# Dealing the prepared projection's steps by its handovers, and two more PSUM banks for the last logits

## The chip, the cores and the metric

One core of one Trainium2 chip runs the whole program. The metric is device time in microseconds of one launch, as the median of repeated runs. The engines are named as in the profile: PE (TensorE matmuls), PEld (its weight loads), DVE (VectorE), ACT (ScalarE), POOL (GpSimd), SP (SyncE, which issues most DMAs and passes some waits on).

## The reference

The input x has 2048 rows of 512 numbers. Four layers follow each other, A, B, A, B, each as `x = x + layer(layernorm(x))`, with 32 heads of 16 numbers. What matters here is layer B: attention inside four segments of 512 rows, with a memory that is carried from segment to segment.

```
def _A_ref(x, wqkv, w_phi, wo):          # linear attention with a learned feature map
    q, k, v = split(x @ wqkv)
    phi(t) = concat(softmax(t @ w_phi), softmax(-(t @ w_phi)))
    o = phi(q) (phi(k)^T v) / (phi(q) sum(phi(k)) + 1e-6)
    return o @ wo

def _B_ref(x, wq, wk, wv, wo, beta):
    for s in range(4):                   # segments of 512 rows
        qs, ks, vs = q[:, :, s], k[:, :, s], v[:, :, s]
        logits = einsum("bhqd,bhkd->bhqk", qs, ks) * scale + mask    # causal
        a_dot = softmax(logits) @ vs
        a_mem = (phi(qs) @ M) / (phi(qs) @ z + 1e-6)
        outs.append(g * a_mem + (1.0 - g) * a_dot)
        M = M + phi(ks)^T vs;  z = z + sum(phi(ks))
    return concat(outs) @ wo
```

## The kernel before

The kernel keeps float32 values as two parts, a high part rounded to the matmul's type and a low rest (hi and lo; hh and hl, oh and ol are such pairs), and multiplies three of the four combinations. Every instruction is issued from helpers, so line numbers are those of the helpers: L154 for DVE, ACT, POOL and SP, L176 for matmuls (`mm`), L180 for transposes (`tp`). Instructions run on each engine in the order in which the program writes them.

Layer B (`class LayerB`) works in 32 groups m, four heads of one segment each, and `steps` runs through them in rounds of a loop over k. A group takes R = 5 rounds; k = 0 to 159 are the rounds proper. In each round:

- `attend` puts the logits of one part of group m = k // 5 into PSUM, exponentiates them on ACT into a tile P (six buffers), and has POOL set the entries beyond the diagonal to zero (`affine_select`). The logits take two banks, one for each half e of the rows; the tile is `lg`, and there is one of it. It is 4 matmuls for the rounds k % 5 = 2, 3 and 4, and 2 for the others.
- `maxima` does the products from which the maxima of a later group are taken, into the banks `mx` and `my` (or two of the four `g` buffers). It runs LEAD = 9 rounds ahead, so the last of it is before k = 151. The last transposed maxima (`put_maxima`) use `mx` at k = 150.
- at k % 5 = 0, `weighted` multiplies the tiles P of the group before by v (`g<-P,v`), and `finish` brings an earlier group's result back to rows.

Beside this, each round has a slot of other work from a table, one per kind of segment: FIRST, GAPS, and for the last segment LAST (first layer B) or FINAL (second layer B). An entry such as `6.2 P/6` stands for k = 120 + 6·5 + 2 = 152 and means six steps of the generator `early`. A `v/1` in LAST is one step of the following layer A's first pass.

`early` is the prepared projection: the last segment's rows are projected with wo for the three quarters of the heads that are done, so that only the last quarter is left behind the loop. It goes in two halves of two row tiles each. A half is `pre` or `pt` steps (loads, transposes, the pair oh and ol from them, in two buffers each), and then 18 steps of `mm3_pair`. A step is two matmuls side by side, one on rows 0 to 63 of the array and one on rows 64 to 127. The two halves of the rows take turns at the two banks: steps 1 to 4 one way, 5 to 13 the other, 14 to 18 the first way again. At such a change the first matmul waits for the last of the turn before. This goes through SP, as a no-operation that waits for the matmul and signals back:

```
                if first and step > 0 and row == 0:
                    after(i, passed)
            if step + 1 < len(steps) and steps[step + 1][4]:
                passed = sync.nop(nofuse=True)
                after(passed, i)
```

These are the handovers: behind the 4th and the 13th step of each half. In the table before, a slot of six steps (k = 152, 153, 154) has the first handover inside the slot of 152 and the second inside that of 154. At k = 156 to 159 the slots had 4, 5, 5 and 4 steps in LAST and 4, 3, 3 and 2 in FINAL, where the last six steps come behind the loop: four behind the last group's `finish`, the others behind the transposes of `end_turn`, which then casts into the same two buffers oh. `thin` is true in the second layer B alone.

Of the kernel before, what the change touches and what calls it, by code (L numbers as in the profile page):

```python
# [10 lines left out]
AF = mybir.ActivationFunctionType  # L11
# [7 lines left out]
P = 128  # L19
NSEG = 4  # L20
# [12 lines left out]
R = 5  # L33
# [46 lines left out]
3.0 max turn turn fin ln | 3.1 O/6     | 3.2 O/6           | 3.3 O/6 | 3.4 O/6  # L80
4.0 max ln ln a2 fin a2 | 4.1 v/2      | 4.2 v/2           | 4.3 v/2 | 4.4 v/2
5.0 max a3 a3 fin | 5.1 v/2           | 5.2 v/2           | 5.3 v/2 | 5.4 v/2
6.0 max fin pre | 6.1 pt pt         | 6.2 P/6           | 6.3 P/6 | 6.4 P/6 v/1
7.0 max pt pt fin | 7.1 P/4           | 7.2 P/5 v/1       | 7.3 P/5 v/1 | 7.4 P/4 v/2
"""
FINAL = """
0.0 max a1 a1 fin | 0.1 Q2/6          | 0.2 Q2/6          | 0.3 Q2/6 | 0.4 Q2/6
# [2 lines left out]
3.0 max a2 a2 fin | 3.1 O/6           | 3.2 O/6           | 3.3 O/6 | 3.4 O/6  # L90
4.0 max turn turn fin | 4.1 O/6        | 4.2 O/6           | 4.3 O/6 | 4.4 O/6
5.0 max a3 a3 fin | 5.1 O/6           | 5.2 O/6           | 5.3 O/6 | 5.4 O/6
6.0 max fin pre | 6.1 pt pt         | 6.2 P/6           | 6.3 P/6 | 6.4 P/6
7.0 max pt pt fin | 7.1 P/4           | 7.2 P/3           | 7.3 P/3 | 7.4 P/2
"""
BEFORE = {-25: "load q0", -24: "sq0 sq1", -23: "k0", -22: "sk0 n n", -21: "sk1 v0/2 n n", -20: "v0/2 n n",
          -19: "n n", -18: "v1 n n q1/2", -17: "q1/2", -16: "k1/2", -15: "k1/2", -11: "v2", -9: "max0"}
# [3 lines left out]
def interleave_kernel(ctx, tc, x_in, a_wqkv, a_wphi, a_wo, b_wq, b_wk, b_wv, b_wo, b_beta,  # L101
# [13 lines left out]
    def nm(s):  # L115
        uid[0] += 1
        return f"{s}_{uid[0]}"

    def T2(tag, bufs, dt=F32, shape=(P, 512)):
        return sp.tile(list(shape), dt, tag=tag, bufs=bufs, name=nm(tag))  # L120

    def PS(tag, bufs, shape=(P, 512)):
        return ps.tile(list(shape), F32, tag=tag, bufs=bufs, name=nm(tag))
# [38 lines left out]
    dve, act, pool, sync = [Ordered(e) for e in (nc.vector, nc.scalar, nc.gpsimd, nc.sync)]  # L162

    def held(i):

        if last[0] is not None:
            behind(i, last[0])
        last[0] = i
        return i
# [3 lines left out]
    def mm(*a, **k):  # L173
        n = a[0].free_size()
        work[0] += n / 2.26 if k["rhs"].dtype == F32R else (n * 2 / 2.4 + 25 if "tile_position" in k else 2 * max(112, n * 2 / 2.4))
        return held(nc.tensor.matmul(*a, **k))  # L176
# [803 lines left out]
    class LayerB:  # L980
# [211 lines left out]
        def attend(self, m):  # L1192


            s, c, hf = m // 8, m % 8 // 2, m % 2
            Q, K = [t[:, 2 * hf : 2 * hf + 2, :] for t in self.st[s, c]["set"]]
            self.pr[m] = {}

            def prod(pb, r, kb, at, w):
                for e in range(2):  # L1200
                    q, k = Q[64 * e : 64 * e + 64, r, :], K[64 * e : 64 * e + 64, r, :]
                    mm(pb[:, e, at : at + w], lhsT=k[:, kb * P : (kb + 1) * P],
                       rhs=q[:, 512 - w : 512], start=True, stop=True, tile_position=(64 * e, 0))

            for kbs, r in (((0,), 0), ((0,), 1), ((1, 3), 0), ((1, 3), 1), ((2,), None)):
                pb = PS("lg", 1, (P, 2, 512))
                pr = T2("P4", NP4, shape=(P, 2, 512))
                pq = pr.rearrange("p e (b x) -> p e b x", b=4)
                if kbs == (0,):
                    prod(pb, r, 0, 0, 512)  # L1210
                    diags = [pr[:, :, 0:P]]
                elif kbs == (1, 3):
                    prod(pb, r, 3, 256, 256)
                    prod(pb, r, 1, 0, 384)
                    diags = [pq[:, e, 0:4:3, :] for e in range(2)]
                else:
                    for rr in range(2):
                        prod(pb, rr, 2, 256 * rr, 256)
                    diags = [pr.rearrange("p e (r x) -> p (e r) x", r=2)[:, :, 0:P]]
                self.pr[m][kbs, r] = pr  # L1220
                with tc.high_priority():
                    act.activation(pr, pb, AF.Exp, scale=0.25)
                for diag in diags:
                    pool.affine_select(out=diag, in_=diag, pattern=[[0, diag.shape[1]], [1, P]],
                                            compare_op=ALU.is_ge, fill=0.0, base=0, channel_multiplier=-1)
                yield
# [327 lines left out]
```

## Time and profile before

| | |
|---|---|
| median of 3 runs | 1360.74 us (1359.96 to 1362.49) |
| profiled execution | 1361.73 us |
| its span, first to last instruction | 1360.0 us |
| PE busy | 1317.2 us, 97% of the span |
| DVE, ACT, POOL busy | 76%, 59%, 51% |
| exponentials of logits, P<-lg | 320 of 1030 ns each |
| granted PE clock, mean | 0.999 |

A row of a timeline gives the start in us from the span's beginning, the time that the row covers, the engine, the line, the operation, output<-input, and in brackets the idle time of the engine ahead of it with what released it. Rows that are alike and follow each other are merged (x4). A matmul's own duration is longer than the distance to the next one, since they overlap in the array; distances between starts are what PE's throughput is read from. In the chain that ended last, "issue" is time in which the engine waited for nothing that the profile shows. The end of the first layer B's loop lies at about 670 to 695 us, that of the second at 1327 to 1347.

### The profile page before, as it was taken

What the parts mean: (1) busy time and instruction counts of PE and PEld (TensorE: products, weight loads), DVE (VectorE), ACT (ScalarE), POOL (GpSimd) and SP (SyncE); (2) the same over time, 40 slices, a digit from 0 to 9 for tenths busy, and PEclk for the clock granted to TensorE, in tenths of its full rate; (3) what the DMA queues carried; (4) which work ended last, traced back from release to release, by engine and by line L of the source; (5) the groups of instructions that cost most, each with busy time, mean ns of one, the idle gap of its engine ahead of it and who ended that gap; (6) DMA issues with size and microseconds to landing.
All of it is one profiled execution on the core that took longest, in us unless ns stands there. A gap on an engine that the chain in (4) does not pass through costs nothing.

```text
span 1360.0 us, 36811 instructions
## 1 busy us (share of the span) xinstructions
PE 1317.2 (97%) x14056; PEld 1028.9 (76%) x14056; DVE 1040.3 (76%) x3256; ACT 808.7 (59%) x1201; POOL 696.9 (51%) x1060
## 2 busy tenths in 40 slices
PE   7999989999999999999999998999999999999997
PEld 6888868777777877777768886786777787787764
DVE  4766778777888888888657677887778879878882
ACT  5556345547677677677544433453766866866654
POOL 1568666326447557345324356553356656654442
PEclk9999999999999999999999999999999999999999
DMA  6388447535654544546251103755555554544441
GB/s 205 102 325 278 157 132 231 173 97 140 173 167 131 158 117 134 153 120 182 87 181 37 63 33 126 241 164 132 143 163 164 152 157 99 150 130 98 118 116 42
DMA packets 134400, 196.27 MB, mean 144 GB/s; under 512 B 15440, under 2 KB 61648, under 8 KB 133456
## 3 DMA queue, kind: packets, MB, share of 16 engines
q1 hardware_dynamic: 132256, 193.27, 48.8%
q8 instruction: 112, 1.84, 0.6%
q10 hardware_dynamic: 1968, 0.64, 0.2%
q14 instruction: 64, 0.52, 0.1%
HBM read 101.05 MB, written 39.85 MB: 104 GB/s over the span
## 4 chain that ended last, share of the span: by engine, by line
PE 76%; DVE 11%; ACT 4%; issue 3%; POOL 3%; DMA 1%; SPq 0%; ACTq 0%; DVEq 0%; POOLq 0%
PE g L176 58%; PE lg L176 6%; PE g L180 6%; PE mx L176 3%; ACT P L154 2%; POOL P L154 2%; DVE g L154 2%; PE lg L180 2%; PE my L176 1%; DVE es L154 1%; POOL tb L154 1%; DVE my L154 1%; DVE mx L154 1%; DVE mxs L154 1%; PE mx L180 1%
## 5 line engine op out<-in xcount | busy, mean ns | idle before, releaser
L154 ACT ACTIVATE P<-lg 128x1024 f32<-128x1024 f32 x320 | 329.6, 1030 | 171.4 <-PE lg L176 93.8
L154 POOL TENSOR_SCALAR_AFFINE_SELECT P<-P 128x256 f32<-128x256 f32 (+1 forms) x448 | 193.4, 446 | 285.7 <-ACT P L154 284.0
L154 DVE CUSTOM_DVE_ANT_0 g<-g,mask 128x256 f32<-128x256 f32 (+3 forms) x392 | 191.6, 545 | 8.6 <-PE g L176 8.3
L176 PE MATMUL g<-hh,wqk 64*128 64x512 f32 (+1 forms) x960 | 186.5, 392 | 0.5 <-DMA wqk<-wqk 0.3
L176 PE MATMUL g<-w,oh 64*128 64x512 f32 (+2 forms) x880 | 177.7, 384 | 1.3 <-DVE ol L154 0.7
L154 DVE CUSTOM_DVE_ANT_0 mx<-mx,mask 128x512 f32<-128x512 f32 (+2 forms) x316 | 158.0, 500 | 21.3 <-PE my L176 17.6
L154 DVE CUSTOM_DVE_ANT_0 my<-my,mask 128x512 f32<-128x512 f32 (+2 forms) x316 | 164.1, 519 | 0.0
L176 PE MATMUL lg<-e,e 64*128 64x256 f32 (+2 forms) x1024 | 153.1, 339 | 4.1 <-ACT P L154 4.1
L176 PE MATMUL g<-P,v 128*32 128x128 f32 (+3 forms) x2064 | 151.1, 433 | 3.6 <-DVE mxs L154 3.0
L176 PE MATMUL g<-w,hh 64*128 64x512 f32 (+1 forms) x672 | 143.9, 395 | 2.0 <-ACT w L154 1.3
L154 DVE DVE_READ_ACCUMULATOR2_ANT mxs<- 128x1 f32 x1024 | 145.3, 142 | 0.0
L176 PEld LDWEIGHTS lg<-e,e 64*128 64x128 f32 x1024 | 102.1, 185 | 35.2 <-issue 11.3
L176 PEld LDWEIGHTS g<-P,v 128*32 128x32 f32 x2064 | 61.2, 109 | 87.5 <-issue 60.8
L176 PEld LDWEIGHTS g<-w,oh 64*128 64x128 f32 (+1 forms) x880 | 107.0, 186 | 18.5 <-SPq L154 3.0
L176 PEld LDWEIGHTS g<-hh,wqk 64*128 64x128 f32 (+1 forms) x960 | 105.6, 185 | 17.2 <-PE my L176 1.0
L154 POOL TENSOR_SCALAR tb<-tb 128x512 f32<-128x512 f32 x72 | 109.2, 1528 | 16.0 <-ACT tb L154 16.0
L176 PE MATMUL g<-w,ol 64*128 64x512 f32 (+2 forms) x440 | 115.6, 377 | 0.0
L176 PE MATMUL g<-hl,wqk 64*128 64x512 f32 (+1 forms) x480 | 106.2, 391 | 0.2
L176 PEld LDWEIGHTS g<-w,hh 64*128 64x128 f32 (+1 forms) x672 | 84.4, 187 | 16.1 <-ACT w L154 1.6
L154 ACT COPY tb<-g 128x512 f32<-128x512 f32 (+1 forms) x132 | 71.2, 576 | 42.7 <-PE g L176 40.8
L176 PE MATMUL g<-w,hl 64*128 64x512 f32 (+1 forms) x336 | 90.1, 392 | 0.0
L154 DVE TENSOR_REDUCE es<-P 128x64 f32<-128x1024 f32 x64 | 77.4, 1209 | 12.9 <-ACT P L154 12.9
(149 smaller groups left out, 2887.9 us busy)
## 6 DMA issues: line engine op xcount, KB each, us to landing
e<-ta SPq DMA_DIRECT2D x384, 128.0 KB
wqk<-wqk SPq DMA_DIRECT2D x128, 256.0 KB
x<-x SPq DMA_DIRECT2D x48, 256.0 KB
ot<-in SPq DMA_DIRECT2D x26, 256.0 KB
pq<-tb SPq DMA_DIRECT2D x24, 256.0 KB
tb<-pq SPq DMA_DIRECT2D x24, 256.0 KB
x<-xr SPq DMA_DIRECT2D x22, 256.0 KB
xr<-x SPq DMA_DIRECT2D x20, 256.0 KB
```

The lines of the kernel that those rows point to most:

```text
L154: i = f(*a, **k)
L176: return held(nc.tensor.matmul(*a, **k))
L180: return held(nc.tensor.transpose(*a))
```

## The change

The slots of the last two blocks in LAST and FINAL get other numbers of steps: 4, 9 and 5 at k = 152, 153 and 154 in both. At k = 156 to 159 LAST has 4, 5, 4 and 5, and FINAL 4, 5, 4 and none. So each handover now falls between two slots, with the logits of the next round written in between. In FINAL 13 steps instead of 12 lie inside the loop.

In the second layer B, the rounds k = 153, 155, 157 and 159 put their logits into `mx` and `my` instead of `lg`, and exponentiate the two banks by two instructions of 512 elements each.

```
-6.0 max fin pre | 6.1 pt pt         | 6.2 P/6           | 6.3 P/6 | 6.4 P/6 v/1
-7.0 max pt pt fin | 7.1 P/4           | 7.2 P/5 v/1       | 7.3 P/5 v/1 | 7.4 P/4 v/2
+6.0 max fin pre | 6.1 pt pt         | 6.2 P/4           | 6.3 P/9 | 6.4 P/5 v/1
+7.0 max pt pt fin | 7.1 P/4           | 7.2 P/5 v/1       | 7.3 P/4 v/1 | 7.4 P/5 v/2
...
-7.0 max pt pt fin | 7.1 P/4           | 7.2 P/3           | 7.3 P/3 | 7.4 P/2
+7.0 max pt pt fin | 7.1 P/4           | 7.2 P/5           | 7.3 P/4 | 7.4
...
-                    mm(pb[:, e, at : at + w], lhsT=k[:, kb * P : (kb + 1) * P],
+                    mm(pb[e][:, at : at + w], lhsT=k[:, kb * P : (kb + 1) * P],
...
-                pb = PS("lg", 1, (P, 2, 512))
+                apart = self.thin and self.k > 8 * R * NSEG - 9 and self.k % 2
+                if apart:
+                    pb = [PS(t, 1) for t in ("mx", "my")]
+                else:
+                    both = PS("lg", 1, (P, 2, 512))
+                    pb = [both[:, e] for e in range(2)]
...
-                    act.activation(pr, pb, AF.Exp, scale=0.25)
+                    for out, src in ([(pr[:, e], pb[e]) for e in range(2)] if apart else [(pr, both)]):
+                        act.activation(out, src, AF.Exp, scale=0.25)
```

On PE, in the first layer B at k = 158 and 159, the handover (from the rows `w_4966,ol` to the rows `w_4967,oh` of the prepared projection, tiles g_10432 and g_10433) stood ahead of layer A's step (g_10465) and the logits lg:

```order
 L176 MATMUL g_10433<-w_4966,ol_10403 128x512
 L176 MATMUL g_10432<-w_4966,ol_10401 128x512
-L176 MATMUL g_10432<-w_4967,oh_10400 128x512
-L176 MATMUL g_10433<-w_4967,oh_10402 128x512
 L176 MATMUL g_10465<-e_1898_10365,hh_9449 128x512
 L176 MATMUL g_10465<-e_1899_10366,hh_9449 128x512
 L176 MATMUL g_10465<-e_1898_10365,hl_9450 128x512
-L176 MATMUL lg_10505<-e_450_2824,e_451_2825 128x256 x4
+L176 MATMUL lg_10503<-e_450_2824,e_451_2825 128x256 x4
+L176 MATMUL g_10432<-w_4967,oh_10400 128x512
+L176 MATMUL g_10433<-w_4967,oh_10402 128x512
```

The step behind the handover has moved behind the logits.

On PE, in the second layer B at k = 152 and 153, the same with the new banks; the first handover is where g_20165 is followed by g_20165 again:

```order
 L176 MATMUL g_20164<-w_14902,oh_20139 128x512
-L176 MATMUL g_20165<-w_14902,oh_20141 128x512 x2
+L176 MATMUL g_20165<-w_14902,oh_20141 128x512
+L176 MATMUL mx_20175<-e_2263_12760,e_2264_12761 128x256
+L176 MATMUL my_20176<-e_2263_12760,e_2264_12761 128x256
+L176 MATMUL mx_20175<-e_2263_12760,e_2264_12761 128x384
+L176 MATMUL my_20176<-e_2263_12760,e_2264_12761 128x384
+L176 MATMUL g_20165<-w_14902,oh_20141 128x512
 L176 MATMUL g_20164<-w_14902,oh_20139 128x512
```

The logits of k = 153 now stand at the handover, in mx and my.

On PE, behind the second loop, from the middle of the leftover steps to the first matmul of the last quarter (before; tmp are the last heads' rows that `end_turn` transposes):

```order
-L176 MATMUL g_20280<-w_14902,oh_20248 128x512
-L176 MATMUL g_20281<-w_14902,oh_20250 128x512
-L180 MATMUL g_20390<-ident,tmp_19924 128x128 x2
-L180 MATMUL g_20397<-ident,tmp_19924 128x128 x2
-L176 MATMUL g_20280<-w_14903,oh_20248 128x512
-L176 MATMUL g_20281<-w_14903,oh_20250 128x512
-L176 MATMUL g_20280<-w_14902,ol_20249 128x512
-L176 MATMUL g_20281<-w_14902,ol_20251 128x512
-L176 MATMUL g_20406<-w_14902,oh_20388 128x512
```

The same place in the changed kernel:

```order
+L176 MATMUL g_20284<-w_14903,oh_20252 128x512
+L176 MATMUL g_20285<-w_14903,oh_20254 128x512
+L180 MATMUL g_20400<-ident,tmp_19924 128x128 x2
+L180 MATMUL g_20407<-ident,tmp_19924 128x128 x2
+L176 MATMUL g_20284<-w_14902,ol_20253 128x512
+L176 MATMUL g_20285<-w_14902,ol_20255 128x512
+L176 MATMUL g_20414<-w_14902,oh_20398 128x512
```

The last step that reads the old oh (`w_14903,oh`) has moved from behind the transposes to ahead of them; one step is left behind them.

More of the change, by code (lines that the diff above doesn't have):

```diff
@@ L92 @@
 5.0 max a3 a3 fin | 5.1 O/6           | 5.2 O/6           | 5.3 O/6 | 5.4 O/6
-6.0 max fin pre | 6.1 pt pt         | 6.2 P/6           | 6.3 P/6 | 6.4 P/6
-7.0 max pt pt fin | 7.1 P/4           | 7.2 P/3           | 7.3 P/3 | 7.4 P/2
+6.0 max fin pre | 6.1 pt pt         | 6.2 P/4           | 6.3 P/9 | 6.4 P/5
+7.0 max pt pt fin | 7.1 P/4           | 7.2 P/5           | 7.3 P/4 | 7.4
 """
```

## The prediction

> **What bounds the kernel now.** I read the page first, for the shares and the chain that ended last, then the chain in order of time, then the timelines of TensorE (PE), its weight loads, ScalarE (ACT) and VectorE (DVE) at the ends of the two loops.
>
> ```profile
> PE 1317.2 (97%) x14056; PEld 1028.9 (76%) x14056; DVE 1040.3 (76%) x3256; ACT 808.7 (59%) x1201; POOL 696.9 (51%) x1060
> PE 76%; DVE 11%; ACT 4%; issue 3%; POOL 3%; DMA 1%; SPq 0%; ACTq 0%; DVEq 0%; POOLq 0%
> ```
>
> PE is busy 97% of the span and carries 76% of the chain, so a stretch can only be shortened where PE waits. The first such place is the last block of rounds (k = 156 to 159). The chain there is logits, exponential, logits, exponential:
>
> ```profile
> 1342.46 1.03 ACT P L154
> ...
> 1343.54 0.58 PE lg L176 x4
> ...
> 1344.23 1.03 ACT P L154
> ```
>
> One turn from exponential to exponential takes 1344.23 - 1342.46 = 1.77 us, because the next logits go into the one pair of banks (lg) that the exponential is still reading. PE has less work than that per round:
>
> ```profile
> 1340.12 0.50 PE L176 MATMUL lg<-e,e 64*128 64x512 f32 x2
> ...
> 1341.24 0.59 PE L176 MATMUL g<-w,oh 64*128 64x512 f32 x2
> 1341.80 0.56 PE L176 MATMUL lg<-e,e 64*128 64x256 f32 x4
> 1342.20 0.63 PE L176 MATMUL g<-w,oh 64*128 64x512 f32 x4
> 1342.66 0.41 PE L176 MATMUL g<-w,ol 64*128 64x512 f32 x2
> 1343.54 0.56 PE L176 MATMUL lg<-e,e 64*128 64x256 f32 x4 [0.47 <-ACT P L154]
> ...
> 1344.40 0.39 PE L176 MATMUL g<-w,ol 64*128 64x512 f32 x2
> 1345.31 0.51 PE L176 MATMUL lg<-e,e 64*128 64x256 f32 x4 [0.51 <-ACT P L154]
> 1345.65 0.63 PE L176 MATMUL g<-w,oh 64*128 64x512 f32 x4
> 1346.21 2.37 PE L176 MATMUL g<-P,v 128*32 128x256 f32 x48
> ```
>
> A step of the prepared projection is two matmuls side by side; steps follow each other every 0.23 us (1342.20 to 1342.66 is two). So k = 158's logits could start at 1342.66 + 0.23 = 1342.89 and start at 1343.54: 0.65 us lost. k = 159's lose 1345.31 - 1344.63 = 0.68. k = 157's lose some 0.2.
>
> The second place is the handover inside a step pair, where the halves change banks through a wait that SyncE passes on:
>
> ```profile
> 1334.00 0.44 PE L176 MATMUL lg<-e,e 64*128 64x256 f32 x4
> 1334.28 0.39 PE L176 MATMUL g<-w,ol 64*128 64x512 f32 x2
> 1334.77 0.50 PE L176 MATMUL g<-w,oh 64*128 64x512 f32 x2
> 1335.11 0.40 PE L176 MATMUL g<-w,ol 64*128 64x512 f32 x2
> ```
>
> From the last step before it to the first behind it is 0.49 us instead of 0.23, and the next step follows after 0.34 instead of 0.23, since the array has run empty. A handover in the open costs 0.26 + 0.11, about 0.36 us. These are the ones in the open at both ends; the weight loads show what they waited for:
>
> ```profile
> 675.91 0.30 PEld L176 LDWEIGHTS g<-w,oh 64*128 64x128 f32 x4 [0.53 <-SPq L154]
> 678.96 0.19 PEld L176 LDWEIGHTS g<-w,oh 64*128 64x128 f32 x2 [0.42 <-SPq L154]
> 690.11 0.19 PEld L176 LDWEIGHTS g<-w,oh 64*128 64x128 f32 x2 [0.52 <-SPq L154]
> ```
>
> ```profile
> 1331.73 0.30 PEld L176 LDWEIGHTS g<-w,oh 64*128 64x128 f32 x4 [0.53 <-SPq L154]
> 1334.77 0.19 PEld L176 LDWEIGHTS g<-w,oh 64*128 64x128 f32 x2 [0.41 <-SPq L154]
> ```
>
> The third place is the tail behind the loop, where a handover and the leftover steps stand between the last head's transposes and the casts:
>
> ```profile
> 1349.60 0.51 PE L176 MATMUL g<-w,ol 64*128 64x512 f32 x2
> 1350.20 0.50 PE L176 MATMUL g<-w,oh 64*128 64x512 f32 x2
> ...
> 1351.09 0.66 PE L180 MATMUL g<-ident,tmp 128*128 128x128 f32 x4
> 1351.68 0.50 PE L176 MATMUL g<-w,oh 64*128 64x512 f32 x2
> 1352.02 0.39 PE L176 MATMUL g<-w,ol 64*128 64x512 f32 x2
> 1353.10 0.73 PE L176 MATMUL g<-w,oh 128*128 128x512 f32 x2 [0.69 <-DVE ol L154]
> ```
>
> ```profile
> 1352.21 0.65 ACT L154 CAST oh<-g 128x256 fp32r<-128x256 f32 x2 [3.03 <-PE g L176]
> ```
>
> ```profile
> 1350.39 0.29 DVE L154 TENSOR_TENSOR tmp<-tmp,wt 128x128 f32<-128x128 f32 x1
> ...
> 1352.62 0.76 DVE L154 TENSOR_TENSOR ol<-g,oh 128x256 fp32r<-128x256 f32 x2 [1.93 <-ACT oh L154]
> ```
>
> The cast waits for PE g of L176, not for the transposes (L180): there are two buffers oh, and the step at 1351.68 (ending 1352.18) is the last that reads the old oh. The next matmuls, at 1353.10, wait for the ol that follows the cast.
>
> **The change part by part.** First, the deal of steps in the first loop's end (times near 680). The number of matmuls is the same; only places change. The handovers at 675.91, 678.96 and 690.11 move behind the next round's logits. Those take 0.29 us on PE (1334.00 to 1334.28) after the last step's 0.23: 0.52, and the handover needs 0.49, so the cover just holds; without it 0.36 each comes back. Gain 3 x 0.36 = 1.08. One thing is late next: k = 155's logits come 0.72 earlier, but k = 154's exponential, still on lg, comes only some 0.1 earlier, and takes back about 0.18. Sum: -0.90. SyncE's order is unchanged; the eight loads of the next pass's weights that stand in its queue behind the second handover are released earlier with it. After this loop PE runs on with few waits, so the gain should arrive at the end; bounds 0 and 1.08.
>
> Second, block 6 of the second loop (k = 152 to 154): handovers at 1331.73 and 1334.77 go the same way. Here k = 153 and 155 write to mx and my, whose last use by the maxima lies before k = 151, so no logits wait. Gain 2 x 0.36 = 0.72; bounds 0.5 and 0.8.
>
> Third, block 7 (k = 156 to 159). Without waits PE would save 0.2 + 0.65 + 0.68, some 0.3 more because logits in a stream take 0.29 and not the 0.40 of 1341.80 to 1342.20, and pay 0.23 for a thirteenth step: 1.5 net. The selections on POOL come late next. In times of before less 0.72: k = 157's logits at 1340.85, its five steps from 1341.22 (the handover's 0.49 behind the fourth), k = 158's logits at 1342.39, their exponential from about 1342.94 to 1343.97, then these two kinds of selection:
>
> ```profile
> 1345.32 0.77 POOL L154 TENSOR_SCALAR_AFFINE_SELECT P<-P 128x256 f32<-128x256 f32 x2 [1.00 <-ACT P L154]
> 1347.03 0.64 POOL L154 TENSOR_SCALAR_AFFINE_SELECT P<-P 128x512 f32<-128x512 f32 x1 [0.94 <-ACT P L154]
> ```
>
> The first ends near 1344.80; the weighting (g from P and v) needs it 0.56 after its start, an estimate from 12 of its 48 matmuls in 2.37 us. It would be there at 1344.5, so it waits 0.3: at that matmul 1344.84 against 1346.77 before, 1.93 less. The second ends near 1345.8, before its matmuls at 1346.0. Less the 0.72 above, this block gives -1.20; bounds 0.5 and 1.5.
>
> Splitting four exponentials in two costs ACT little by the nearest row, two 512-wide casts that follow each other:
>
> ```profile
> 1303.82 1.03 ACT L154 CAST oh<-g 128x512 fp32r<-128x512 f32 x2
> ```
>
> That is the 1.03 of one 1024-wide exponential. I take 0.05 per split, hidden where ACT waits for PE; the upper bound is 0.4, if the halves do not overlap, and then the last selection would hold the weighting by some 0.3, inside the bounds above.
>
> The Trainium skill (ScalarE: Activation LUTs, What ACT_TABLE_LOAD costs) speaks against a split: an ACTIVATE with immediate operands costs a fixed 186 ns beside its elements, of which about 93 ns overlaps with the next. By that each pair costs 0.09 us more than one; k = 158's exponential still starts by its logits, so the sum would be the same within 0.1. The exponential of 1.03 us agrees with the page's 1.04 for 1024 elements; no run here yet shows a split.
>
> Fourth, the tail. Five steps are left instead of six, and the handover lies behind us: the four steps ahead of the transposes lose the 0.6 - 0.23 of 1349.60 to 1350.20, so the transposes start 0.36 earlier, as the last tmp on DVE (1350.39 + 0.29 = 1350.68) just allows. Behind them only an ol step is left. The first cast no longer waits for it, but the first ol does: with transposes at 1350.73 on the old scale, that step runs 1351.32 to 1351.82, ol follows at 1351.87 and not 1352.62. Gain -0.75; bounds 0.36 (the handover alone) and 1.0 (ol free too). What follows (twelve matmuls, four additions, stores) moves with it.
>
> Sum: -0.90 - 0.72 - 1.20 - 0.75 = -3.57 us. The profiled execution took 1361.73 and would take 1358.2 (span 1356.4); it lies 1 us above the median of the runs, 1360.74, from which the forecast goes: 1357.2.
>
> **The rivals.** (1) The first loop's gain is swallowed before the end, because something later is paced by DMA. For it: eight weight loads follow in SyncE's queue. Against: the page gives DMA 1% of the chain. Then -2.67: 1358.1.
>
> (2) The last block is held by ACT and POOL, at the low bounds of the third and fourth parts (0.5, 0.36): -0.90 - 0.72 - 0.50 - 0.36 = -2.5: 1358.3.
>
> (3) The change does not do what it says: PE still waits in block 7 as now, since the cover of 0.52 against 0.49 fails and the split exponentials hold mx as long as lg was held. Then only the first loop, block 6 and the tail's 0.36 remain: -2.0: 1358.8.
>
> (4) Slower. The instruction streams of ACT and PE get longer in the last rounds, and a wait for issue could fall into the last block, where nothing covers it. Such waits stand in the trace elsewhere:
>
> ```profile
> PE my L176 <- issue: 3.9, 2, 2.2
> ```
>
> Two of the longest, 4.4 us, turn the sum to +0.8: 1361.6; with three it is slower beyond doubt, 1363.8. It decides from 1.6 stalls on. Against it: both lie in another stage, none in any of the last rounds.
>
> **How the numbers follow.** About 0.2%, 2.7 us, is what a measurement of this kernel can tell from no change; three runs of before lie 2.5 apart. Chances: forecast 0.60, (1) 0.15, (2) 0.12, (3) 0.08, (4) 0.05. The line at 1358.0 runs close to (1) and (2): of the forecast 0.56 falls below it, of (1) to (3) 0.12. Faster 0.68, same 0.27, slower 0.05. The range takes the upper bounds (-1.08 - 0.8 - 1.5 - 1.0 = -4.4, 1356.4) with half a microsecond of spread, and upward reaches past (3): 1355.9 to 1359.6.
>
> **What would show it.** In the profile of the changed kernel: no weight load of these steps waits for SPq in either end; logits under mx and my at odd rounds from k = 153 with no idle time behind ACT; one short wait for POOL inside the last weighting; the last cast released by the transposes of L180, ol by the step behind them; block k = 156 to the weighting about 4.6 us instead of 6.1. Wrong would be: idle time before lg or mx of over 0.3 us in that block, a cast that still waits for L176, or the second layer starting no earlier than now.

## The result, and the profile after

| | before | changed | ratio, 95% interval |
|---|---|---|---|
| first measurement, 9 runs each | 1362.44 us | 1358.73 us | 0.9971 [0.9962, 0.9981] |
| second measurement, 21 and 12 runs | 1362.07 us | 1360.16 us | 0.9984 [0.9975, 0.9994] |
| profiled execution, span | 1361.73, 1360.0 us | 1357.14, 1355.4 us | |

The changed kernel is faster by two to three thousandths. The forecast was 1357.2 us, 3.57 us less than before. The two intervals overlap between 0.9975 and 0.9981, which is 2.6 to 3.4 us. The first measurement's medians lie 3.71 us apart, nearer to 3.57 than the parts of the change add up to below, 3.08; so that nearness is partly luck.

The page of the changed kernel, busy time of PE and shares of the chain, moves little beside that of before:

```profile
PE 1315.4 (97%) x14056; PEld 1032.6 (76%) x14056; DVE 1039.5 (77%) x3256; ACT 808.6 (60%) x1205; POOL 695.8 (51%) x1060
PE 74%; DVE 10%; ACT 5%; issue 4%; POOL 3%; DMA 3%; SPq 1%; ACTq 0%; DVEq 0%; POOLq 0%
```

What is to be seen are the four more instructions on ACT, the split exponentials. The two profiled spans lie 4.6 us apart, and that is not all the change. These are PE's timelines around the changed stretches (start, time covered, engine, line, operation, output<-input, shapes, count). First before, at the first loop's end, then its rows in the second loop that were not shown yet (the count of the weighting is cut by the window):

```profile
674.03 1.10 PE L176 MATMUL g<-w,oh 64*128 64x512 f32 x4
...
694.40 1.93 PE L176 MATMUL g<-P,v 128*32 128x512 f32 x24
...
1329.85 1.11 PE L176 MATMUL g<-w,oh 64*128 64x512 f32 x4
...
1348.51 0.44 PE L180 MATMUL g<-ident,U 128*128 128x128 f32 x2
```

Then the changed kernel, at the same places:

```profile
671.83 1.11 PE L176 MATMUL g<-w,oh 64*128 64x512 f32 x4
...
691.40 2.36 PE L176 MATMUL g<-P,v 128*32 128x512 f32 x32
...
1327.54 1.11 PE L176 MATMUL g<-w,oh 64*128 64x512 f32 x4
...
1331.38 0.39 PE L176 MATMUL g<-w,ol 64*128 64x512 f32 x2
1331.61 0.40 PE L176 MATMUL lg<-e,e 64*128 64x256 f32 x4
1331.88 0.50 PE L176 MATMUL g<-w,oh 64*128 64x512 f32 x2
1332.21 0.39 PE L176 MATMUL g<-w,ol 64*128 64x512 f32 x2
1332.44 0.63 PE L176 MATMUL g<-w,oh 64*128 64x512 f32 x4
...
1337.22 0.50 PE L176 MATMUL lg<-e,e 64*128 64x512 f32 x2
...
1340.30 0.45 PE L176 MATMUL lg<-e,e 64*128 64x256 f32 x4
...
1341.84 2.87 PE L176 MATMUL g<-P,v 128*32 128x256 f32 x48
1344.64 0.44 PE L180 MATMUL g<-ident,U 128*128 128x128 f32 x2
...
1347.42 0.50 PE L176 MATMUL g<-w,ol 64*128 64x512 f32 x2
1348.51 0.74 PE L176 MATMUL g<-w,oh 128*128 128x512 f32 x2 [0.58 <-DVE ol L154]
```

The first changed instruction comes after 674.03 in the one and 671.83 in the other: 2.20 us of the difference arise where both kernels issue the same instructions. Between the loops (694.40 to 1329.85, 691.40 to 1327.54) the changed kernel takes 636.14 instead of 635.45, 0.69 more. Neither belongs to the change. What does can be cut into four stages, from start to start of the same matmuls:

| stage | before | changed | difference | forecast |
|---|---|---|---|---|
| A: first loop, first step at k = 152 to the last weighting | 20.37 | 19.57 | -0.80 | -0.90 |
| B: second loop, first step at k = 152 to k = 156's logits | 10.27 | 9.68 | -0.59 | -0.72 |
| C: from there to the transposes of U | 8.39 | 7.42 | -0.97 | -1.20 |
| D: from there to the last quarter's first matmul | 4.59 | 3.87 | -0.72 | -0.75 |
| sum | 43.62 | 40.54 | -3.08 | -3.57 |

-3.08 - 2.20 + 0.69 = -4.59: the spans' difference is accounted for. Behind stage D nothing moves: from the last quarter's first matmul to the end of the program it is 6.88 to 6.91 us in every trace of this case. Of the time before, -3.08 us is 0.23%, a ratio of 0.9977, inside the first interval and inside the second.

Now the engines beside PE in the changed kernel's last block and tail: the weight load that waits, ACT, DVE and POOL.

```profile
1341.84 0.72 PEld L176 LDWEIGHTS g<-P,v 128*32 128x32 f32 x14
1342.79 1.44 PEld L176 LDWEIGHTS g<-P,v 128*32 128x32 f32 x34 [0.22 <-POOL P L154]
```

```profile
1329.55 0.60 ACT L154 ACTIVATE P<-mx 128x512 f32<-128x512 f32 x1 [0.75 <-PE mx L176]
1330.04 0.59 ACT L154 ACTIVATE P<-my 128x512 f32<-128x512 f32 x1
...
1340.88 1.03 ACT L154 ACTIVATE P<-lg 128x1024 f32<-128x1024 f32 x1 [0.62 <-PE lg L176]
1342.01 0.60 ACT L154 ACTIVATE P<-mx 128x512 f32<-128x512 f32 x1
...
1347.31 0.65 ACT L154 CAST oh<-g 128x256 fp32r<-128x256 f32 x2 [2.03 <-PE g L180]
```

```profile
1348.03 0.76 DVE L154 TENSOR_TENSOR ol<-g,oh 128x256 fp32r<-128x256 f32 x2 [1.22 <-PE g L176]
```

```profile
1341.97 0.76 POOL L154 TENSOR_SCALAR_AFFINE_SELECT P<-P 128x256 f32<-128x256 f32 x2 [1.24 <-ACT P L154]
1343.22 0.63 POOL L154 TENSOR_SCALAR_AFFINE_SELECT P<-P 128x512 f32<-128x512 f32 x1 [0.49 <-ACT P L154]
```

In this stretch (the second loop's last two blocks and the tail) the view of waits, which counts waits above 0.15 us, has no weight load behind SPq and no matmul into lg, mx or my behind ACT: both of the losses that the prediction read are gone there. ACT, which before came round once in 1.77 us, now runs k = 158's and 159's exponentials almost one into the other (1340.88 + 1.03 = 1341.91, next at 1342.01). What ends last in the block is POOL's selection: it ends at 1341.97 + 0.76 = 1342.73, and the weight loads go on at 1342.79. In the tail the cast is released by the transposes (L180), and ol by the one step behind them.

### The profile page after: what moved, and what is told of

Read it like the earlier page. It is cut to its first block, busy times and chain, and to the rows that moved or that the text cites. A ratio compares the mean times of both kernels' runs of the same rounds, so it can differ in the third digit from the quotient of the medians.

```text
span 1355.4 us, 36817 instructions
## 1 busy us (share of the span) xinstructions
PE 1315.4 (97%) x14056; PEld 1032.6 (76%) x14056; DVE 1039.5 (77%) x3256; ACT 808.6 (60%) x1205; POOL 695.8 (51%) x1060
## 4 chain that ended last, share of the span: by engine, by line
PE 74%; DVE 10%; ACT 5%; issue 4%; POOL 3%; DMA 3%; SPq 1%; ACTq 0%; DVEq 0%; POOLq 0%
PE g L176 56%; PE lg L176 6%; PE g L180 6%; PE mx L176 3%; ACT P L154 3%; POOL P L154 2%; DVE g L154 2%; PE lg L180 2%; SPq L154 1%; POOL tb L154 1%; PE my L176 1%; DMA x<-x 1%; DVE es L154 1%; PE mx L180 1%; DVE my L154 1%
## 5 line engine op out<-in xcount | busy, mean ns | idle before, releaser
L154 ACT ACTIVATE P<-lg 128x1024 f32<-128x1024 f32 x316 | 325.4, 1030 | 167.1 <-PE lg L176 92.5
L176 PE MATMUL lg<-e,e 64*128 64x512 f32 (+1 forms) x1010 | 152.0, 339 | 3.1 <-ACT P L154 3.1
```

The lines of the kernel that those rows point to most:

```text
L154: i = f(*a, **k)
```

## The experiments

A total of one run says little here, since executions of the same program lie up to 7 us apart (before, in one measurement of 35 runs: 1358.86 to 1365.79 us). The stages do say something: a stage is taken from each trace as above, from start to start of the same matmuls.

| kernel | A | B | C | D | sum against before | ratio from the sum | measured ratio |
|---|---|---|---|---|---|---|---|
| before, again | 20.37 | 10.27 | 8.39 | 4.59 | 0.00 | 1.0000 | 1.0002 [0.9990, 1.0015] |
| first loop's deal alone | 19.56 | 10.26 | 8.39 | 4.59 | -0.82 | 0.9994 | 0.9993 [0.9982, 1.0005] |
| second loop's deal alone | 20.36 | 9.85 | 8.17 | 3.88 | -1.36 | 0.9990 | 0.9994 [0.9982, 1.0006] |
| banks alone | 20.38 | 10.21 | 6.96 | 4.57 | -1.50 | 0.9989 | 0.9988 [0.9977, 1.0000] |
| changed, again | 19.60 | 9.69 | 7.42 | 3.87 | -3.04 | 0.9978 | 0.9984 [0.9975, 0.9994] |
| two amendments | 19.57 | 9.69 | 6.96 | 3.56 | -3.84 | 0.9972 | 0.9974 [0.9963, 0.9984] |
| three amendments | 19.27 | 9.69 | 6.96 | 3.56 | -4.14 | 0.9970 | 0.9969 [0.9957, 0.9981] |

The measured ratios follow the sums. Only the intervals of the lower four end at a ratio of 1 or below it; for the two deals by themselves the totals cannot be told from before, and the stages have to decide.

**The kernel before, once more.** No edit.

> The kernel before, unchanged, as a control of the timing and of the granted clock from run to run. Theory (four local gains, and single executions that differ by a couple of microseconds for reasons that have nothing to do with the change): a ratio of 1 within 0.1 to 0.15%, and clocks between 0.995 and 0.999, as the changed kernel's runs had. Rival (the changed kernel costs clock: its runs show 0.995 to 0.998 where the profiled execution of before shows 0.999): every run here at 0.999.

1362.40 us against 1361.77; its four stages equal those of the first profile to 0.01 us, and its clocks are 0.994 to 0.998, so the lower clock is not the change's. So a stage is read to hundredths from one trace, while its span (1363.2) lies 3.2 us above the first one's.

**The first loop's deal alone.**

```
-6.0 max fin pre | 6.1 pt pt | 6.2 P/6 | 6.3 P/6 | 6.4 P/6 v/1               (LAST)
-7.0 max pt pt fin | 7.1 P/4 | 7.2 P/5 v/1 | 7.3 P/5 v/1 | 7.4 P/4 v/2
+6.0 max fin pre | 6.1 pt pt | 6.2 P/4 | 6.3 P/9 | 6.4 P/5 v/1
+7.0 max pt pt fin | 7.1 P/4 | 7.2 P/5 v/1 | 7.3 P/4 v/1 | 7.4 P/5 v/2
```

> The new deal of steps in the first loop alone. Stretch A, from the first step at k = 152 to the weighting behind k = 159 in the first loop (20.37 us before, 19.57 in the changed kernel): 19.57. The second loop's stretches as before: B, first step at k = 152 to the logits of k = 156: 10.27; C, from there to the transposes of U: 8.39; D, from there to the first matmul of the last quarter: 4.59. Total -0.8 us. Rival (the first loop's gain is swallowed by the pass that follows): A 19.57, but the total unchanged.

1361.51 us. Stage A falls by 0.81, the rest stays. The gain is not swallowed by what follows. From the loop's last weighting to products of `my` that start 139 us later (694.40 to 833.28 before, 691.40 to 830.25 in the changed kernel), all thirteen traces take 138.83 to 138.94 us, with the old deal and the new one. Only behind that do they part, at a wait of PE of 1.7 to 3.9 us (last section). Over the whole stretch between the loops the five kernels with A as before mean 636.1 us (635.4 to 637.6), the eight with the new deal 635.8 us (635.0 to 636.7).

**The second loop's deal alone**, and **the banks alone.** The first is the kernel before with this edit; the second is the changed kernel with the old slots in both tables.

```
-6.0 max fin pre | 6.1 pt pt | 6.2 P/6 | 6.3 P/6 | 6.4 P/6                   (FINAL)
-7.0 max pt pt fin | 7.1 P/4 | 7.2 P/3 | 7.3 P/3 | 7.4 P/2
+6.0 max fin pre | 6.1 pt pt | 6.2 P/4 | 6.3 P/9 | 6.4 P/5
+7.0 max pt pt fin | 7.1 P/4 | 7.2 P/5 | 7.3 P/4 | 7.4
```

> The new deal in the second loop alone, logits all in lg. Theory: the logits stay bound to the exponential's turn of 1.75 us, so block 7 gains little: A 20.37, B about 9.75 (k = 155's logits wait some 0.15 for k = 154's exponential), C about 8.0 (the two steps that stood behind the last logits are gone from there, their time goes into waits that stood there anyway), D 3.87 (handover and oh step out of the tail). Total -1.6. Rival (the deal is what carries the gain and the banks add nothing): B 9.68, C 7.42, D 3.87, total -2.3.

> The two more banks in the second loop alone, old deals of steps. Theory: block 6 has no logits that wait, so B stays 10.27 with both handovers in the open; in block 7 no logits wait, and with only 12 steps the weighting starts some 1.8 us earlier: C about 6.6, which is less than the changed kernel's 7.42, since there the selections come late; D stays 4.59, with the handover and the last oh step in the tail. Total -1.8. Rival (a split exponential costs ACT a fixed price, and ACT and POOL then hold the weighting): C 7.5 or more.

1361.54 and 1360.55 us. The deal owns D (-0.71) and most of B (-0.42); the waits of logits for the exponential ahead of them remain, and in its stretch the view of waits (us in total, times, longest) has

```profile
PEld lg L176 <- ACT P L154: 1.9, 4, 0.7
```

The banks alone take 1.43 us out of C and leave the handovers where they were (timeline of PE, then waits). C came to 6.96 and not to the 6.6 expected: the weighting starts 4.39 us behind k = 156's logits, 1.70 earlier than before, but takes 2.57 us instead of 2.30.

```profile
1342.37 0.50 PE L176 MATMUL lg<-e,e 64*128 64x512 f32 x2
...
1346.76 2.64 PE L176 MATMUL g<-P,v 128*32 128x256 f32 x48
1349.33 0.44 PE L180 MATMUL g<-ident,U 128*128 128x128 f32 x2
```

```profile
PEld g L176 <- SPq L154: 1.4, 3, 0.5
```

The parts do not add up in C: -1.43 and -0.22 by themselves, -0.97 together. With the banks, the new deal of the last block costs 0.46 us there. Four more experiments, of one run each, go after the sizes; their totals (1360.55, 1364.71, 1359.50 and 1360.33 us, in the order told) are within the spread of the 35 runs above, so only their stages are read.

**A handover put back in the open**, in block 6 of FINAL: `6.2 P/5 | 6.3 P/8 | 6.4 P/5` instead of 4, 9 and 5.

> The changed kernel with one handover put back into the open: 5, 8 and 5 steps at k = 152 to 154 of the second loop instead of 4, 9 and 5. Theory (a handover costs what the array stands empty for, the logits between cover it): stretch B 9.68 + 0.3 = 9.98, the rest as in the changed kernel (C 7.42, D 3.87). Rival (block 6 got shorter by the banks, not by where the handover lies): B 9.68.

```profile
1330.69 1.11 PE L176 MATMUL g<-w,oh 64*128 64x512 f32 x4
...
1340.65 0.50 PE L176 MATMUL lg<-e,e 64*128 64x512 f32 x2
```

Stage B is 1340.65 - 1330.69 = 9.96 instead of 9.68: an open handover costs 0.28 more than a covered one. The changed kernel's rows show why it is not 0.36. From 1331.38 the items ol, lg, oh, ol take 1.06 us (to 1332.44); before, the items lg, ol, oh, ol took 1334.00 to 1335.35, which is 1.35. The 0.26 of waiting is covered, but the step behind the handover still needs 0.33 (1331.88 to 1332.21) instead of 0.23 to its follower: most of the 0.11 stays. The cover only just held. The weight load of that step starts at 1331.87, with its matmul and 0.49 behind the last step before the handover, as late as in the open; it could not run ahead of its matmul. With a longer cover it does, and then the 0.11 goes too (the first loop's third handover, below).

**Twelve steps in the loop instead of thirteen**, in the changed kernel: `7.3 P/3` instead of `7.3 P/4`.

> The changed kernel with 12 steps in the second loop instead of 13 (4, 5 and 3 at k = 156 to 158), so that the second handover and an oh step fall back into the tail. Theory: D back to 4.59; C stays near 7.42, since the weighting begins 0.23 earlier but waits for the same selections, which hang on k = 158's logits behind five steps. Rival (the tail got shorter because one step fewer is left, 0.23): D 4.1.

C stays at 7.42 and D is 4.56. The weighting starts 4.39 us behind k = 156's logits instead of 4.62, and takes 3.03 instead of 2.80: what comes earlier is waited away. So the thirteenth step costs nothing inside the loop, because the block waits for something else, and it is worth 0.69 us behind it. In this execution stage A reads 19.97, though that part is unaltered; a stretch of half clock lies in it (last section).

**The same thirteen steps dealt 4, 3, 3, 3** instead of 4, 5, 4 and none.

> The changed kernel with the 13 steps dealt 4, 3, 3 and 3 over k = 156 to 159 instead of 4, 5, 4 and none. Theory (the last weighting waits 0.5 us for the selection of k = 158, which hangs on k = 158's logits): those logits come two steps, 0.47 us, earlier, the wait goes, PE's work is the same, C 7.42 - 0.47 = 6.95; B and D unchanged. Rival (the weighting is held by the exponentials' split or by POOL's own pace): C 7.42.

```profile
1339.99 0.50 PE L176 MATMUL lg<-e,e 64*128 64x512 f32 x2
...
1342.60 0.45 PE L176 MATMUL lg<-e,e 64*128 64x256 f32 x4
...
1344.62 2.39 PE L176 MATMUL g<-P,v 128*32 128x256 f32 x48
1346.94 0.44 PE L180 MATMUL g<-ident,U 128*128 128x128 f32 x2
```

C is 6.95. k = 158's logits start 2.61 us behind k = 156's and not 3.08 as in the changed kernel (1340.30 - 1337.22): 0.47 earlier, and 0.47 is what C gains. The weighting starts no earlier (4.63 behind k = 156's logits, 4.62 in the changed kernel), but runs in 2.32 instead of 2.80. So in the changed kernel C is paced by one chain: k = 158's logits, their exponential, the selection, the weighting that needs it. That also explains the experiment before: twelve steps leave the nine ahead of those logits as they are. With 4, 3, 3, 3 the weighting takes as long as before the change (2.30), so nothing is left to wait for there.

**The tail's high and low parts in buffers of their own**, in the kernel before.

```
-    def turn(ot):
-
-        o = [T2("oh", OO, F32R), T2("ol", OO, F32R)]
+    def turn(ot, tags=(("oh", OO), ("ol", OO))):
+
+        o = [T2(*tag, F32R) for tag in tags]
...
-            return [turn([last[:, t], last[:, t + 1]]) for t in (0, 2)]
+            tags = ((("ta1", TA),) * 2,) if self.thin else ()
+            return [turn([last[:, t], last[:, t + 1]], *tags) for t in (0, 2)]
```

> The kernel before, with the last casts writing into buffers of their own (the eight of ta1, long free) instead of the two of oh and ol; deals and banks as before. Theory (the casts waited for the last step that reads the old oh): the cast follows the transposes, D 4.59 - 0.65 = 3.94, with the handover still in the tail. Rival (the casts waited for PE to come through its steps in order, or the additions on DVE bind): D 4.59.

```profile
1347.74 0.44 PE L180 MATMUL g<-ident,U 128*128 128x128 f32 x2
...
1351.70 3.06 PE L176 MATMUL g<-w,ta 128*128 128x512 f32 x12
```

```profile
1350.82 0.65 ACT L154 CAST ta<-g 128x256 fp32r<-128x256 f32 x2 [2.40 <-PE g L180]
```

```profile
1351.22 0.76 DVE L154 TENSOR_TENSOR ta<-g,ta 128x256 fp32r<-128x256 f32 x2 [1.30 <-ACT ta L154]
```

D is 1351.70 - 1347.74 = 3.96, with all six steps still behind the loop. What held the tail was the pair of buffers: with other buffers the cast follows the transposes, and the subtraction follows its cast by 0.40 us. Before, the cast waited for the last reader of oh.

**The findings put together.** The changed kernel measured again beside two versions that these experiments point to: 4, 3, 3, 3 with the tail's own buffers, and that with `apart` freed of `self.thin`, so that the first loop alternates banks as well.

> The changed kernel itself, unaltered, once more beside the kernel before. If the stages' durations belong to the program, it shows 19.58 us from the first loop's k = 152 to its last weighting, 9.68 us for the sixth block of the second loop, 7.42 us from the logits of k = 156 to the transposes of U, and 3.87 us from there to the last quarter's first matmul, each within 0.05 us, and a ratio near 0.997 to 0.998. If those sizes were an accident of one execution, they move by several tenths.

> The changed kernel with both amendments of the looks: thirteen steps in the last block dealt 4, 3, 3, 3, and the end's high and low parts in buffers of their own. If the two are independent, the stages read 19.58, 9.68, 6.95 and 3.55 us: the weighting 0.47 us earlier, and the last quarter's first matmul 0.32 us earlier, because the subtraction follows its cast by 0.40 us (as in the look at buffers of their own) and not by 0.72 us. Together 0.8 us less than the changed kernel, about 1357.5 us. Rival: the end gains nothing, because with twelve matmuls instead of thirteen behind the transposes the wait is for the cast alone; the last stage stays at 3.87 us.

> As the kernel with both amendments, and the last products of the first loop alternate with the maxima's banks as well. If the first loop's logits still wait for the exponential before them, its stage falls from 19.58 us by the 0.15 to 0.2 us that the trace of the changed kernel shows there, to about 19.4 us; the rest reads 9.68, 6.95 and 3.55 us. Rival: the dealt steps already cover that wait, and splitting the exponentials only adds 0.05 us a pair to the scalar engine: 19.58 us or a little over.

1360.16, 1358.88 and 1358.28 us, ratios in the table. C and D come out as expected. Banks in the first loop bring 0.30, more than the 0.15 to 0.2 expected; in the changed kernel that stretch had

```profile
PEld lg L176 <- ACT P L154: 0.7, 2, 0.4
```

and with the banks this wait is gone. By the stages this last version is 1.06 us faster than the changed kernel. The totals agree in order, but their intervals overlap.

## Why the prediction was right, and where its sizes were off

**The second layer's tail, -0.75: measured -0.72.** The steps held as described: cast released by the transposes, ol by the ol step behind them. With buffers of its own as well, the stage is 1.03 shorter than before, where the prediction had its bound for ol free too, 1.0.

**Block 6, -0.72: measured -0.59.** The step that failed is "2 x 0.36", by the cover of 0.52 against 0.49 that "just holds". It was enough for the wait of 0.26; the weight load behind the handover still starts 0.49 behind the last step, with its matmul and not ahead of it, and most of the 0.11 stayed. By the experiment with the open handover it is 0.28 each.

**The first loop, -0.90: measured -0.80.** The term "3 x 0.36" was too large here too, but for two of the three handovers alone. Between the same steps on both sides of it, the first saved 0.29 (674.76 to 676.78 before, 672.55 to 674.28 in the changed kernel) and the second 0.28 (678.18 to 679.53, and 675.67 to 676.74). The third saved its whole 0.36 (first fence before, second changed):

```profile
689.63 0.39 PE L176 MATMUL g<-w,ol 64*128 64x512 f32 x2
...
691.78 0.41 PE L176 MATMUL g<-w,ol 64*128 64x512 f32 x2
```

```profile
687.00 0.40 PE L176 MATMUL g<-w,ol 64*128 64x512 f32 x2
...
688.56 0.40 PE L176 MATMUL g<-w,oh 64*128 64x512 f32 x2
688.79 0.40 PE L176 MATMUL g<-w,ol 64*128 64x512 f32 x2
```

The same matmuls take 2.15 us before and 1.79 in the changed kernel. Here layer A's step and the logits lie in the handover, 1.56 us instead of 0.49; the weight load behind it starts at 688.44, 0.12 ahead of its matmul, and the next step follows after 0.23. The 0.18 taken back by k = 155's logits came as forecast: from k = 154's last step to the weighting it is 0.72 us (677.20 to 677.92) instead of 0.55 (680.00 to 680.55), 0.17 more. 0.29 + 0.28 + 0.36 - 0.17 makes 0.76 of the 0.80. What the logits of this loop still wait shows elsewhere: alternating banks there were worth 0.30.

**Block 7, -1.20: measured -0.97.** The mechanism was the right one, a wait that moves from the banks to POOL's selection, and the start of the weighting came where it was put: 4.62 us behind k = 156's logits, forecast "about 4.6 instead of 6.1". The term that was mis-sized is what the wait inside the weighting costs. From its start to the transposes of U it takes 2.80 us instead of 2.30 (1346.21 to 1348.51 before), 0.50 and not 0.3. The first selection ended 5.51 us behind k = 156's logits and not 5.40. Fourteen weight loads run ahead of it, and the fifteenth matmul starts at 1342.79, 0.95 behind the weighting's start instead of 0.58: the wait is 0.37, near the forecast. From there to U it takes 1.85 us, and 1.72 before: 0.13 that the prediction had not, since it took the rest as unchanged. The start came 0.08 later than by its own working (1344.5 - 0.56 - 1339.40 = 4.54). These make up the 0.23 within rounding. The second selection ended at 1343.22 + 0.63 = 1343.85, 6.63 behind k = 156's logits and not 6.40, but it held nothing: in the kernels with banks alone and with twelve steps it ended 1.0 us ahead of U instead of 0.79, and the fifteenth matmul to U took 1.85 there as well. Why the matmuls behind such a wait take 0.13 more stays open. Two readings are off without touching the forecast: by the rows shown k = 157's logits lost 1341.80 - 1341.47 = 0.33 and not 0.2, and the terms of "1.5 net" add up to 1.6; both enter the bound alone.

**The split, 0.05 a pair.** The halves take 1330.04 + 0.59 - 1329.55 = 1.08 us, against 1.03 for one of 1024: 0.05, the size that the prediction took. An estimate from the figures of the Trainium skill (ScalarE: Activation LUTs, What ACT_TABLE_LOAD costs), 186 ns less 93 ns of overlap, is 0.09; the measurement is lower.

**The rivals.** (1), the first loop's gain swallowed, is spoken against by the 139 us behind the loop, which all traces repeat within 0.1 us, and by the stretch between the loops, which is not longer when the first loop is shorter; by totals alone it could not be ruled out. (2) is partly so: ACT and POOL do pace the last block, at -0.97 rather than at its bound of -0.50. The tail is not held. (3) did not occur, since no logits wait for ACT in that block and the cover held for the wait. (4) did not either: no stall for issue of over 0.5 us lies in the last 30 us.

## What to carry to other kernels

Where the total of two runs differs by chance as much as by the change, cut the trace at instructions that both kernels have: a stretch of 4 to 20 us repeats to hundredths of a microsecond, and sums of such stretches lie within the interval of every measured ratio here. When a wait is taken away, find the chain that ends last next, and give work to the engine only behind the start of that chain: two of the thirteen steps written ahead of k = 158's logits cost 0.47 us, and nothing behind them. Cover a handover by more than it takes: with logits that just filled its 0.49 us, 0.28 of its 0.36 us was saved, with 1.56 us of other work all of it. No run here changes the length of the cover alone.

## What the runs showed of the hardware

A wait of PE of 2 us in the middle of the program was followed by 3.4 us at half clock in one execution, and not in another. Both kernels issue the same instructions here, far from the change; the first fence is before, the second the changed kernel.

```profile
836.50 0.45 PE L176 MATMUL my<-v,P 128*32 128x17 f32 x33 [2.23 <-issue]
836.88 3.06 PE L176 MATMUL g<-e,w 128*128 128x512 f32 x12
```

```profile
833.18 0.45 PE L176 MATMUL my<-v,P 128*32 128x17 f32 x33 [1.95 <-issue]
833.56 4.61 PE L176 MATMUL g<-e,w 128*128 128x512 f32 x12
```

The same twelve matmuls take 3.06 us in the one and 4.61 in the other. The busy time by stretches of 6 us has the granted clock behind the five engines, then the DMA share and GB/s; before first:

```profile
830.00:836.00 6.00, 4.27 (x149) 3.34 (x138) 4.44 (x8) 1.49 (x2) 5.53 (x5) 1.00 0.97 320
836.00:842.00 6.00, 4.36 (x55) 3.51 (x54) 5.19 (x10) 2.79 (x5) 3.15 (x3) 1.00 0.82 284
```

```profile
830.00:836.00 6.00, 4.05 (x137) 3.26 (x136) 3.66 (x9) 2.59 (x3) 4.69 (x6) 0.86 1.05 354
836.00:842.00 6.00, 4.85 (x53) 4.01 (x53) 4.25 (x9) 2.56 (x3) 1.98 (x2) 0.86 0.29 97
```

0.86 over both stretches is 2 x 0.14 x 12 = 3.4 us at half clock (from 834.50 to 837.50 the granted clock reads 0.50 throughout), and it cost 4.61 - 3.06 = 1.55 us. The kernel before, profiled once more, had a mean clock of 0.994, against 0.999 in its first profile, so this is no mark of the change; it is one part of the few microseconds by which executions differ. The Trainium skill (TensorE: Matmul & The Clock Gate, What's actually happening) has a free-running window of 3.4 us, after which an idle array falls to half clock. The length agrees; but the waits here are 1.95 and 2.23 us, shorter than the window, and the longer one kept the full clock.

The traces show what decides between the two. Each stretch at half clock inside a program is 3.413 us long, or twice that, and in each trace all of them begin whole multiples of 3.413 us apart: in the changed kernel at 18.53, 834.32 and 933.30 us, which is 239 and 268 periods behind the first. So the periods run on by themselves. In the changed kernel the wait, 831.23 to 833.18, lies inside one period (830.90 to 834.32). In the kernel before, the wait, 834.27 to 836.50, is cut by the period's end at 835.41, into 1.14 and 1.09 us. Of the thirteen traces, the clock fell behind this wait in the eight in which PE stood idle for 1.88 us or more of one period, and in none of the five in which the most was 1.69. Idle time is not all of it: near 183 us eight traces kept the full clock behind a period with 1.88 to 1.94 us of idle time, and at 933.30 the changed kernel lost it behind one with 0.7. What counts there, and where the rest of the spread comes from, these runs do not settle.
